# Key pieces turned in pairs in separate PSUM rooms, one fixed room for the output's two banks, and GpSimd's sums issued right behind its shares

## The chip, the cores and the metric

The kernel runs on one core of a Trainium2 chip. The metric is the time of one execution on the device in microseconds (us); the median of three runs is 544.29 us (543.98 to 544.59). The engines of the core work beside each other, each through its own instructions in order: TensorE (PE; its weight loads are counted apart as PEld), VectorE (DVE), ScalarE (ACT), GpSimd (POOL) and SyncE (SP), which issues nearly all DMAs.

## The reference

The inputs q, k, v have shape (B, H, S, D) = (2, 8, 576, 64), all in fp32. Attention with a computed bias is followed by two blocks of a mixture-of-experts shape, each without a router:

```python
scores = q @ k.T / sqrt(D)
x = (log1p(|i - j|) / log1p(max(i, 1)))[..., None]
bias = relu(x @ w1 + b1) @ w2            # hidden 32, one bias per head
attn = exp(scores + bias - max); attn /= attn.sum(-1) + 1e-9
y = attn @ v                             # to (1152, 512)
y = ((y @ w_a) * (y @ w_b)) @ w_out      # 512 -> 1536 -> 512
h = y @ w_in                             # 512 -> 1024
s = h * softmax(h)
out = (layernorm(s) * g_ln) @ w_out2     # 1024 -> 512
```

## The kernel before

Nearly every matrix product is made of three: each operand is split into a high part and the rest (`hi`, `lo`), both in the format fp32r, and hi·hi, hi·lo and lo·hi are summed in PSUM (`three`, L123 to L128). The high part is written by ACT, the rest by DVE as a difference.

PSUM has 8 banks. The pool `ps_s` (two buffers of two banks, tag `s`) holds scores, the bias sums `bps` and what lies beside them. `ps_t` (one buffer of two banks, tag `t`) holds turned (transposed) shares `pt` and turned pieces of q and k, `tp_...`. `ps_x` (two buffers of one bank) holds the attention's output `px_u` of one unit.

**The order of the work** is the order of the code: no scheduler moves anything, and each engine runs its instructions in program order. An instruction waits by semaphores for the tiles it reads and writes.

**Prologue** (loop from L511). The bias of a block of 128 rows is made in eight row groups T. `bias_hidden(T)` makes four relus of 128x576 each, on ACT (L360) or DVE (L362) as a letter string of the table HIDDEN says (`a` or `v`). `bias_sums` (L370) multiplies them by w2 on PE; `bias_out` copies the sums out (ACT, L380) and sends them by DMA from SP into the bias tile (L382). Beside it, pieces of q and k are turned by PE (`turn`, L275; a piece is one `piece`, L319) and split by `high` (ACT, L308) and `lower` (DVE, L313 for keys, L317 for queries). Three pieces are left over for the end of the prologue; the queries of the next unit and the keys of the second batch are fetched there by SP (L256, L261).

**Attention** (loop from L615). There are nine units u: eight of 128 rows of one batch, and a last one with the remaining 64 rows of both batches. A unit has four head pairs p, and step m of the loop starts pair m of 36. In a step stand: scores of two heads (L398); the next unit's queries turned; bias-add on DVE (L412) and exp on ACT (L419) of both heads; for the pair of the step before, `summed_powers`, a GpSimd instruction (sum + 1e-9, L424) and a DVE reciprocal of it (L425); then its `shares` on GpSimd (two multiplications of 128x576, L430); for the pair two steps before, the turning of its shares (L447) and the copies of them (L452, L461); the sums of a later row group T; `values` (L479) for the pair three steps before; the relus of T+1. After a unit's last pair ACT writes the high part of its output (xhi, L485), and one step later DVE the rest (xlo, L490). The first steps also turn the five key pieces of batch 1, at the end of steps 1, 1, 2, 2 and 3, one after another through `ps_t`. In steps 27 and 29 GpSimd clears rooms for the last unit's queries (`clear_q`, L285); from step 28 on the first weights of the next block are brought in and split (`first_one`: ACT L94 and L586, GpSimd L98 and L588, DVE L107, L109, L110).

**After attention** come the two other blocks (gated products `pm`, `po`, then `ph`, `pl`, `py`). The change does not touch them.

Of the kernel before, what the change touches and what calls it, by code (L numbers as in the profile page):

```python
# [17 lines left out]
P = 128  # L18
# [7 lines left out]

LAG = 2

HIDDEN = (("vvva", "vava", "vvva", "vavv", "vvva", "vavv", "vvva", "vavv"), ("vvav", "vvvv", "vavv", "vvva"))

LOADS = ((0, 1), (1, 1), (2, 2), (3, 2))
FIRST = ((-7, -5, -4, -1, 0, 1), (-6, -4, -2, 1, 2, 3), (-5, -2, 0, 3, 4, 5), (0, 2, 4, 6, 7, 8))
# [18 lines left out]
def tile_kernel(ctx, tc, q, k, v, w1, b1, w2, w_a, w_b, w_out, w_in2, w_out2, g_ln, psi, rpsi, out):  # L51
# [108 lines left out]
    with ExitStack() as actx:  # L160
# [6 lines left out]
        etp = actx.enter_context(tc.tile_pool(name="etp", bufs=2))  # L167
        sp = actx.enter_context(tc.tile_pool(name="sp", bufs=4))
        ps_t = actx.enter_context(tc.tile_pool(name="ps_t", bufs=1, space=PSUM))
        ps_x = actx.enter_context(tc.tile_pool(name="ps_x", bufs=2, space=PSUM))  # L170


        tabs = ac.tile([P, UW + NG], F32, name="tabs")
# [34 lines left out]
            return halves  # L208

        halves_r = table(half, UW - half, psi_r, half - 12, ps_s, "s")  # L210
        ps_nb = ps_x.tile([P, 4, NG // 4], F32, tag="x", name="ps_nb")
        for g in range(4):
            nc.tensor.matmul(ps_nb[g * HID:(g + 1) * HID], b1r, psi_i[:, :, g::4], start=True, stop=True)
        nc.scalar.copy(*halves_r[0])
# [5 lines left out]

        def scales():

            ps = ps_x.tile([P, 4, NG // 16], F32, tag="x", name="ps_rp")
            for c in range(4):
                for qd in range(4):
                    nc.tensor.matmul(ps[32 * qd:32 * qd + 32, c], order4[:, c].rearrange("p g h -> p (g h)"), rp_in[:, qd::4], start=True, stop=True)
            nc.scalar.copy(rp.rearrange("p (c k) -> p c k", c=4), ps)
# [78 lines left out]
        def high(views, by=1.0):  # L306
            for hi, _, ps in views:
                nc.scalar.activation(hi, ps, AF.Copy, scale=by)  # L308
# [7 lines left out]
                for l_, p_, h_ in parts_:  # L316
                    nc.vector.scalar_tensor_tensor(out=l_, in0=p_, scalar=by, in1=h_.bitcast(F32), op0=ALU.mult, op1=ALU.subtract)  # L317

        def piece(w, pool=ps_t, tag="t"):  # L319

            src, at, g, c = w
            ps = pool.tile([P, 2, 512], F32, tag=tag, name=f"tp_{'_'.join(map(str, w))}")
            nat = fetched[w]
            if src == "q":
                turn(ps, 0, nat, range(HG))
                return q_views(at, g, 0, ps, 0) + q_views(at, g, 1, ps, 2 * HF), -scale
            turn(ps, 0, nat, range(HG), (0, 1) if c < NK else (at,))
            return k_views(at, g, c, ps, 0), 1.0
# [36 lines left out]
        def bias_sums(T):  # L365

            bps = ps_s.tile([P, 2, 512], F32, tag="s", name=f"bps_{T}")
            for qd, h in enumerate(bias_w[T]):
                for a in range(2):
                    nc.tensor.matmul(bps[32 * qd:32 * qd + 32, a, 0:SH], w2bd, h[:, a * SH:(a + 1) * SH], start=True, stop=True)  # L370
            bias_w[T] = bps
# [49 lines left out]
        def summed_powers(u, p):  # L421
            sums, rec = st_[u]
            heads = slice(2 * p, 2 * p + 2)
            nc.gpsimd.tensor_scalar(rec[:, heads], sums[:, heads], 1e-9, 1.0, op0=ALU.add, op1=ALU.mult)  # L424
            nc.vector.reciprocal(rec[:, heads], rec[:, heads])  # L425

        def shares(u, h):
# [35 lines left out]
        def values(u, p):  # L463

            it, bs = units[u]
            if p == 0:
                st_["x", u] = ps_x.tile([P, HP, P], F32, tag="x", name=f"px_{u}")
            px = st_["x", u]
            et, ett = st_.pop(("et", u, p)), st_.pop(("ett", u, p))
            n = P // len(bs)  # L470
            for c in range(NC + 1):
                for j, part in ((j, part) for j in range(2) for part in range(2)):

                    rows = slice(j * D + part * HID, j * D + (part + 1) * HID)
                    for m, b in enumerate(bs):
                        cols = slice(m * n, (m + 1) * n)
                        lhsT = (vsb[:, b, c] if c < NC else vtl[:, b])[:, p, j, part * HID:(part + 1) * HID]
                        rhs = et[:, j * NC + c, cols] if c < NC else ett[:, cols]
                        nc.tensor.matmul(px[rows, p, cols], lhsT, rhs, start=(c == 0 and m == 0), stop=(c == NC), skip_group_check=True)  # L479
# [31 lines left out]
        for T in range(N0):  # L511
            bias_hidden(T)
            if T > 0:
                bias_sums(T - 1)
                bias_out(T - 1)
            if T == N0 - 2:
                halves_l = table(low, half - low, psi_l, low - 12, ps_t, "t")
            if T == N0 - 1:
                nc.scalar.copy(*halves_l[0])
                nc.vector.tensor_copy(*halves_l[1])  # L520
            if done:
                lower(*done)
                done = None
            if T > 0 and len(order) > 3:
                done = piece(order.pop(0))
                high(*done)
            if T == 1:
                for j in range(2):
                    nc.gpsimd.memset(vtl[(1 - j) * TL:(2 - j) * TL, :, :, j, :], 0.0)
        assert done is None and len(order) == 3  # L530
        bias_sums(N0 - 1)
        bias_out(N0 - 1)
        for w in ks[1][:2]:
            fetch(w)
        for g in range(2):
            fetch(("q", 1, g, 0))
        for p in range(-1, 2):
            load_v(0, p)
        for w in ks[1][2:]:
            fetch(w)  # L540
        for p in range(2, HP):
            load_v(0, p)
        bias_hidden(N0)
        made = piece(order[0])
        high(*made)
        lower(*made)
        made = piece(order[1])
        high(*made)
        lower(*made)
        bias_sums(N0)  # L550
        made = piece(order[2])
        high(*made)
        lower(*made)
        bias_out(N0)

        sums_at, keys_at, extra = {}, {}, {}
# [4 lines left out]
        for T in range(N0 + 1, S // 16):  # L561
            sums_at[T - N0 - 1] = T
        last_sums = max(sums_at)
        for m, w in zip((1, 1, 2, 2, 3), ks[1]):
            keys_at.setdefault(m, []).append(w)
        for p in range(-1, HP):
            later(2 * (2 + max(p, 0)), load_v, 1, p)
# [42 lines left out]
                f(*args)  # L610

        gone = []
        bias_hidden(sums_at[0])
        NP = len(pairs)
        for m in range(NP + LAG + 1):  # L615
            now = pairs[m] if m < NP else None
# [5 lines left out]
            if now:  # L622
                u, p = now
                scores(u, 2 * p)
                spare = scores(u, 2 * p + 1)
                if (u, p) in ((NU - 3, HP - 1), (NU - 2, 1)):
                    clear_q(NU - 1, NU - 2 - u == 0)
            elif up:
                spare = ps_s.tile([P, 2, 512], F32, tag="s", name=f"tails_{m}")
            if up:  # L630
# [7 lines left out]
                biased(u, 2 * p)  # L638
                powers(u, 2 * p)
            if last:  # L640
                summed_powers(*last)
            if now:
                biased(u, 2 * p + 1)
            if up:
                kept_tails(*up, spare)
            high(views, -scale)
# [20 lines left out]
            others(2 * m)  # L667
            if after is not None:
                bias_hidden(after)
            for w in keys_at.get(m, []):  # L670
                made = piece(w)
                high(*made)
                lower(*made)
            if out_ and out_[1] == HP - 1:
                inputs_high(out_[0])
                gone.append(out_[0])
# [345 lines left out]
```

## Time and profile before

| what | value |
|---|---|
| median of three runs | 544.29 us |
| the profiled execution | 545.0 us, of which the span of the trace is 543.2 us |
| PE busy | 510.3 us (94%) |
| DVE, ACT, POOL busy | 404.3, 280.9 and 143.0 us |
| mean granted TensorE clock | 0.971 of full speed |

A row of a timeline gives start, duration, engine, source line, operation, the tile it writes and those it reads, their shapes, the count, and in brackets how long the engine was idle just before it and what ended that. L412 is line 412 of the kernel before.

### The profile page before, as it was taken

The page shows a single profiled execution, that of the slowest core. Times are in us where ns is not written, and L with a number is a line of the kernel's source. Part 1 is how long each engine was busy: PE and PEld are TensorE (multiplying, and loading weights), DVE is VectorE, ACT ScalarE, POOL GpSimd, SP SyncE. Part 2 cuts the span into 40 slices and gives each one's busy share as a digit, 9 for nine tenths or more (in the row PEclk, how much of TensorE's full clock was granted, in tenths as well). Part 3 has the DMA queues.
Part 4 walks back from the last instruction along what each step waited for, and adds up shares of the span by engine and source line. Part 5 has one row for each costly group of instructions (what it writes and reads, how often), then busy time and mean ns, then how long its engine had stood idle before and what let it go on. Part 6 is the DMA issues. An engine that isn't in the chain of part 4 may idle for free.

```text
span 543.2 us, 13461 instructions
## 1 busy us (share of the span) xinstructions
PE 510.3 (94%) x5416; PEld 450.5 (83%) x5416; DVE 404.3 (74%) x880; ACT 280.9 (52%) x610; POOL 143.0 (26%) x216
## 2 busy tenths in 40 slices
PE   6768999999988889899999999999999999999997
PEld 3346777787767779899999999999999988888886
DVE  4777899999965853597899798897884466666561
ACT  5765888898875642455564334522534332232321
POOL 2012333343345560222222122242224330000000
PEclk9966999999988989999999999999999999999999
DMA  5886644434653100744444353445300000000011
GB/s 128 197 183 148 142 109 107 98 102 103 150 141 105 42 3 5 219 136 148 154 139 135 117 156 116 126 147 150 121 1 1 1 1 21 19 21 19 21 39 39
DMA packets 63520, 51.74 MB, mean 95 GB/s; under 512 B 41182, under 2 KB 53731, under 8 KB 63460
## 3 DMA queue, kind: packets, MB, share of 16 engines
q1 hardware_dynamic: 63184, 50.88, 34.8%
q8 instruction: 42, 0.69, 0.6%
q14 instruction: 18, 0.15, 0.1%
q10 hardware_dynamic: 276, 0.02, 0.0%
HBM read 36.73 MB, written 2.36 MB: 72 GB/s over the span
## 4 chain that ended last, share of the span: by engine, by line
PE 69%; DVE 9%; ACT 9%; DMA 4%; issue 4%; SPq 2%; POOL 1%; DVEq 0%; ACTq 0%
PE pm L128 26%; PE po L128 11%; PE py L919 9%; PE ph L859 9%; PE bps L370 4%; ACT e L419 3%; DVE h L362 3%; PE px L479 3%; PE s L398 2%; DMA nat_q<-in_q_dram 2%; PE pl L900 1%; PE pt L447 1%; DMA words<-in_moe_w_out_dram 1%; ACT qhi L308 1%; DVE e L412 1%
## 5 line engine op out<-in xcount | busy, mean ns | idle before, releaser
L128 PE MATMUL pm<-xhi,abh 128*128 128x384 f32 x240 | 80.2, 334 | 0.0
L128 PE MATMUL pm<-xhi,abl 128*128 128x384 f32 x240 | 80.2, 334 | 0.0
L128 PE MATMUL pm<-xlo,abh 128*128 128x384 f32 x240 | 80.2, 334 | 0.0
L98 POOL TENSOR_SCALAR f<-f 128x512 f32<-128x512 f32 x48 | 41.5, 865 | 142.7 <-ACT f L94 136.0
L430 POOL TENSOR_SCALAR e<-e,rec 128x576 f32<-128x576 f32 x72 | 52.9, 746 | 64.5 <-DVE rec L425 58.5
L419 ACT ACTIVATE e<-e,nm 128x576 f32<-128x576 f32 x72 | 56.2, 781 | 23.4 <-DVE rec L425 14.6
L412 DVE CUSTOM_DVE_ANT_0 e<-s,bias 128x576 f32<-128x576 f32 x72 | 53.9, 749 | 5.6 <-PE s L398 3.1
L362 DVE TENSOR_SCALAR h<-tabs 128x576 f32<-128x576 f32 x114 | 51.8, 515 | 0.7 <-PE bps L370 0.6
L370 PE MATMUL bps<-h,w2bd 128*32 128x288 f32 x576 | 47.0, 438 | 3.5 <-DVE nm L412 2.6
L128 PE MATMUL po<-gh,oh 128*128 128x384 f32 x144 | 48.5, 337 | 0.6 <-DVE x2s L790 0.6
L128 PE MATMUL po<-gh,ol 128*128 128x384 f32 x144 | 48.4, 336 | 0.0
L128 PE MATMUL po<-gl,oh 128*128 128x384 f32 x144 | 48.4, 336 | 0.0
L128 PEld LDWEIGHTS pm<-xhi,abh 128*128 128x128 f32 x240 | 45.1, 188 | 0.0
L128 PEld LDWEIGHTS pm<-xlo,abh 128*128 128x128 f32 x240 | 45.1, 188 | 0.0
L128 PEld LDWEIGHTS pm<-xhi,abl 128*128 128x128 f32 x240 | 45.1, 188 | 0.0
L110 DVE SCALAR_TENSOR_TENSOR f<-words,f 128x512 int32<-128x512 int32 x48 | 42.8, 891 | 1.6
L147 ACT COPY one<-pm 128x384 f32<-128x384 f32 x36 | 17.2, 478 | 50.2 <-PE pm L128 50.1
L94 ACT ACTIVATE f<-words 128x512 f32<-128x512 f32 x48 | 32.4, 675 | 18.6 <-DMA words<-in_moe_w_a_dram 7.4
L479 PE MATMUL px<-et,vsb 128*32 128x128 f32 (+1 forms) x1280 | 41.9, 276 | 0.0
L479 PEld LDWEIGHTS px<-et,vsb 128*32 128x32 f32 x1280 | 35.7, 116 | 5.9 <-issue 0.8
L874 ACT ACTIVATE ev<-ph,small 128x512 f32<-128x512 f32 x18 | 12.2, 684 | 49.7 <-DVE small L871 49.6
L109 DVE SCALAR_TENSOR_TENSOR f<-words,f 128x512 int32<-128x512 int32 x48 | 34.1, 710 | 1.3
(148 smaller groups left out, 1212.9 us busy)
## 6 DMA issues: line engine op xcount, KB each, us to landing
bias<-st SPq DMA_DIRECT2D x40, 288.0 KB, 3.7
words<-in_moe_w_out_dram SPq DMA_DIRECT2D x20, 512.0 KB, 3.5
words<-in_moe_w_a_dram SPq DMA_DIRECT2D x12, 512.0 KB, 3.6
words<-in_moe_w_b_dram SPq DMA_DIRECT2D x12, 512.0 KB, 3.8
nat_q<-in_q_dram SPq DMA_DIRECT2D x32, 128.0 KB, 3.5
words<-in_moe_w_in_dram SPq DMA_DIRECT2D x8, 512.0 KB, 3.6
arena<-in_k_dram SPq DMA_DIRECT2D x16, 128.0 KB, 2.6
vsb<-in_v_dram SPq DMA_DIRECT2D x16, 128.0 KB, 3.4
```

Source lines behind the costliest of these rows:

```text
L98: engine.tensor_scalar(f, f, WORD_MAX, WORD_MIN, op0=ALU.min, op1=ALU.max)
L109: nc.vector.scalar_tensor_tensor(out=b, in0=words[:, :, 1], scalar=-0x40000000, in1=b, op0=ALU.bitwise_and, op1=ALU.bitwise_or)
L110: nc.vector.scalar_tensor_tensor(out=b, in0=words[:, :, 0], scalar=29, in1=b, op0=ALU.logical_shift_right, op1=ALU.bitwise_or)
L128: nc.tensor.matmul(ps, w, x, start=(i == 0), stop=(i == n - 1))
L362: nc.vector.tensor_scalar(h, win, sc, 0.0, op0=ALU.add, op1=ALU.max)
L370: nc.tensor.matmul(bps[32 * qd:32 * qd + 32, a, 0:SH], w2bd, h[:, a * SH:(a + 1) * SH], start=True, stop=True)
L412: nc.vector.tensor_tensor_reduce(out=halves(e), in0=ps[:, :, 0:SH], in1=halves(bias_t[it][:, h, :]), op0=ALU.add, op1=ALU.min, scale=1.0, ...
L419: nc.scalar.activation(e, e, AF.Exp, bias=nm, scale=-1.0, accum_out=sums[:, h:h + 1])
L430: nc.gpsimd.tensor_scalar(e, e, rec[:, h:h + 1], 1.0, op0=ALU.mult, op1=ALU.mult)
L479: nc.tensor.matmul(px[rows, p, cols], lhsT, rhs, start=(c == 0 and m == 0), stop=(c == NC), skip_group_check=True)
L859: nc.tensor.matmul(ph[u][:, a], x[:, kc, cols], w[:, kc, a * 512:(a + 1) * 512], start=(i == 0), stop=(i == 3 * KD - 1))
L919: nc.tensor.matmul(ps, x[:, c, :], w[:, c, cols], start=(i == 0), stop=(i == 3 * KF - 1))
```

## The change

1. HIDDEN, the table of who makes which relu, gets other strings. From the second block of rows on, ACT makes four of 16 relus where it made three, two of them in one row group.
2. The pool `ps_x` becomes one fixed tile `xx` of two banks. Unit u's output lies in bank u%2 of it, and it also serves as a room for turned pieces: `piece` takes the name of a room, `t`, `x` or `s`.
3. In the prologue the next unit's queries are fetched earlier (T = 5), the three pieces left over are turned one after another into three rooms before the last bias sums and split behind them, and the relus of row group 9 move from ahead of the attention loop into its first step, behind both bias-adds. Both copies of the left half of the table go to DVE.
4. The key pieces of batch 1 come at steps 0, 0, 1, 1, 2. Their turning stands ahead of `values`, in the rooms `x` and `t`; their split stays at the end of the step.
5. `summed_powers` is split in two. GpSimd's sum is issued in the pair's own step, right behind the shares of the pair before and ahead of `clear_q` and the weights; the reciprocal (`inverted`) stays where it was, on DVE in the next step.

```diff
-HIDDEN = ((..., "vvva", ...), ("vvav", "vvvv", "vavv", "vvva"))
+HIDDEN = ((..., "vava", ...), ("vvvv", "vava", "vvav", "vavv"))
...
-        ps_x = actx.enter_context(tc.tile_pool(name="ps_x", bufs=2, space=PSUM))
+        ps_x = actx.enter_context(tc.tile_pool(name="ps_x", bufs=1, space=PSUM))
+        xx = ps_x.tile([P, 2, 512], F32, tag="x", name="xx")
...
-        def piece(w, pool=ps_t, tag="t"):
+        def piece(w, room="t"):
-            ps = pool.tile([P, 2, 512], F32, tag=tag, name=f"tp_{'_'.join(map(str, w))}")
+            ps = xx if room == "x" else (ps_t if room == "t" else ps_s).tile([P, 2, 512], F32, tag=room, ...)
...
+        def inverted(u, p):
+            _, rec = st_[u]
+            heads = slice(2 * p, 2 * p + 2)
             nc.vector.reciprocal(rec[:, heads], rec[:, heads])
...
-                st_["x", u] = ps_x.tile([P, HP, P], F32, tag="x", name=f"px_{u}")
+                st_["x", u] = xx[:, u % 2].rearrange("p (a t) -> p a t", a=HP)
...
+            if T == N0 - 3:
+                for g in range(2):
+                    fetch(("q", 1, g, 0))
...
-        bias_hidden(N0)
-        made = piece(order[0])
-        high(*made)
-        lower(*made)
-        made = piece(order[1])
-        high(*made)
-        lower(*made)
+        made = [piece(w, room) for w, room in zip(order, "txs")]
         bias_sums(N0)
-        made = piece(order[2])
-        high(*made)
-        lower(*made)
+        for w in made:
+            high(*w)
+            lower(*w)
...
-        for m, w in zip((1, 1, 2, 2, 3), ks[1]):
+        for m, w in zip((0, 0, 1, 1, 2), ks[1]):
...
             if last:
-                summed_powers(*last)
+                inverted(*last)
             if now:
                 biased(u, 2 * p + 1)
+            if m == 0:
+                bias_hidden(T)
...
                     shares(last[0], 2 * last[1] + h)
+            if now:
+                summed_powers(u, p)
+                if (u, p) in ((NU - 3, HP - 1), (NU - 2, 1)):
+                    clear_q(NU - 1, NU - 2 - u == 0)
...
+            made = [piece(w, room) for w, room in zip(keys_at.get(m, []), "xt")]
             if out_:
                 values(*out_)
...
-            for w in keys_at.get(m, []):
-                made = piece(w)
-                high(*made)
-                lower(*made)
+            for w in made:
+                high(*w)
+                lower(*w)
```

On DVE, from the end of the prologue to step 0's first bias-add (`ISA e_0...`), the order was this; `h_0` to `h_3` are relus, `klo` the rest of a key piece:

```order
L362 TENSOR_SCALAR h_3_438<-tabs 128x576
L317 SCALAR_TENSOR_TENSOR qlo_1_0_450<-tp_q_1_0_440,qhi_1_0_449 128x128 x4
L313 TENSOR_TENSOR klo<-tp_k_1_0_457,khi 128x2x4x64
L313 TENSOR_TENSOR klo<-tp_k_1_1_477,khi 128x2x4x64
L362 TENSOR_SCALAR h_0_492<-tabs 128x576
L362 TENSOR_SCALAR h_1_494<-tabs 128x576
L362 TENSOR_SCALAR h_2_496<-tabs 128x576
L362 TENSOR_SCALAR h_3_498<-tabs 128x576
L412 ISA e_0_522,nm_0_523<-s_0_502,bias_209 128x576
```

The same place now:

```order
L363 TENSOR_SCALAR h_3_403<-tabs 128x576
L318 SCALAR_TENSOR_TENSOR qlo_1_0_449<-tp_q_1_0_439,qhi_1_0_448 128x128 x4
L314 TENSOR_TENSOR klo<-xx,khi 128x2x4x64
L314 TENSOR_TENSOR klo<-tp_k_1_1_458,khi 128x2x4x64
L413 ISA e_0_512,nm_0_513<-s_0_492,bias_208 128x576
```

The four relus of row group 9 no longer stand ahead of the first bias-add.

On GpSimd, in steps 27 to 30, the order was this; `rec<-sums` is the sum with 1e-9, `e<-e,rec` two shares, MEMSET the clearing:

```order
L424 TENSOR_SCALAR rec_2848<-sums_2847 128x2
L430 TENSOR_SCALAR e_6_3170<-e_6_3170,rec_2848 128x576 x2
L285 MEMSET qhi_True_3333 128x512
L285 MEMSET qlo_True_3334 128x512
L285 MEMSET qhi_True_3337 128x512
L285 MEMSET qlo_True_3338 128x512
L424 TENSOR_SCALAR rec_3239<-sums_3238 128x2
L430 TENSOR_SCALAR e_0_3260<-e_0_3260,rec_3239 128x576 x2
L98 TENSOR_SCALAR single_3406<-single_3406 128x512
L424 TENSOR_SCALAR rec_3239<-sums_3238 128x2
L430 TENSOR_SCALAR e_2_3347<-e_2_3347,rec_3239 128x576 x2
```

The same place now:

```order
L425 TENSOR_SCALAR rec_3228<-sums_3227 128x2
L435 TENSOR_SCALAR e_0_3249<-e_0_3249,rec_3228 128x576 x2
L425 TENSOR_SCALAR rec_3228<-sums_3227 128x2
L286 MEMSET qhi_True_3343 128x512
L286 MEMSET qlo_True_3344 128x512
L286 MEMSET qhi_True_3347 128x512
L286 MEMSET qlo_True_3348 128x512
L98 TENSOR_SCALAR single_3395<-single_3395 128x512
L435 TENSOR_SCALAR e_2_3328<-e_2_3328,rec_3228 128x576 x2
L425 TENSOR_SCALAR rec_3228<-sums_3227 128x2
L98 TENSOR_SCALAR single_3478<-single_3478 128x512
```

Each sum now stands ahead of the memsets and of the weight work (L98), and the shares of the next pair (`e_2`) stand behind both.

On DVE, at the end of a unit in the fourth step of its period, with the semaphores waited for, the order was this:

```order
L317 SCALAR_TENSOR_TENSOR qlo_1_0_1063<-s_7_1153,qhi_1_0_1062 128x128
L490 TENSOR_TENSOR xlo<-px_789,xhi 128x4x128
L362 TENSOR_SCALAR h_0_1237<-tabs 128x576 [waits DVE_49]
L362 TENSOR_SCALAR h_1_1239<-tabs 128x576 [waits DVE_49]
L362 TENSOR_SCALAR h_2_1241<-tabs 128x576 [waits DVE_49]
```

The same place now:

```order
L318 SCALAR_TENSOR_TENSOR qlo_1_0_1058<-s_7_1148,qhi_1_0_1057 128x128
L495 TENSOR_TENSOR xlo<-xx,xhi 128x4x128 [waits PE_49]
L363 TENSOR_SCALAR h_0_1231<-tabs 128x576 [waits DVE_49]
L363 TENSOR_SCALAR h_2_1235<-tabs 128x576 [waits DVE_49]
L413 ISA e_0_1266,nm_0_1267<-s_0_1244,bias_486 128x576 [waits DMAHW2_49,DMAHW3_49,DMAHW1_49,DMAHW4_49,DMAHW0_49,DMAHW6_49,DVE_49,PE_49]
```

One relu has left DVE there, and xlo now waits for PE: `xx` is followed as one tile, so the reading of one bank waits for the values of the next unit written ahead of it into the other.

## Rows read from the trace of the kernel before

**Rows 1.** The page, part 1: busy time, share and instructions of each engine.

```profile
PE 510.3 (94%) x5416; PEld 450.5 (83%) x5416; DVE 404.3 (74%) x880; ACT 280.9 (52%) x610; POOL 143.0 (26%) x216
```

**Rows 2.** Windows: length, PE, PEld, DVE, ACT, POOL busy, clock, DMA share, GB/s.

```profile
27.60:60.65 33.05, 26.04 (x346) 18.95 (x344) 24.02 (x63) 20.64 (x46) 7.16 (x13) 0.70 0.73 158
60.65:153.42 92.77, 88.76 (x1984) 72.23 (x1984) 87.88 (x250) 83.11 (x199) 37.25 (x67) 1.00 0.50 116
163.13:196.67 33.54, 28.03 (x595) 23.96 (x591) 23.00 (x59) 20.58 (x54) 19.52 (x31) 0.91 0.18 58
196.67:216.00 19.33, 19.33 (x354) 18.17 (x351) 6.70 (x12) 6.60 (x16) 4.27 (x6) 0.98 0.01 3
```

**Rows 3.** Timeline of DVE, end of the prologue to step 4.

```profile
28.51 0.69 DVE L313 TENSOR_TENSOR klo<-tp_k,khi 128x512 fp32r<-128x512 f32 x1 [1.42 <-ACT khi L308]
...
30.84 0.75 DVE L412 CUSTOM_DVE_ANT_0 e<-s,bias 128x576 f32<-128x576 f32 x1
...
35.00 0.76 DVE L412 CUSTOM_DVE_ANT_0 e<-s,bias 128x576 f32<-128x576 f32 x1
...
42.70 0.75 DVE L412 CUSTOM_DVE_ANT_0 e<-s,bias 128x576 f32<-128x576 f32 x1
...
56.77 0.75 DVE L412 CUSTOM_DVE_ANT_0 e<-s,bias 128x576 f32<-128x576 f32 x1
...
60.65 0.75 DVE L412 CUSTOM_DVE_ANT_0 e<-s,bias 128x576 f32<-128x576 f32 x1
```

**Rows 4.** Timeline of all engines, the second key piece of step 1.

```profile
40.72 0.69 PE L275 MATMUL tp_k<-ident,arena 64*128 64x64 f32 x8 [2.57 <-DVE klo L313]
...
41.46 0.60 ACT L308 ACTIVATE khi<-tp_k 128x512 fp32r<-128x512 f32 x1 [1.51 <-PE tp_k L275]
```

**Rows 5.** Timeline of SP, the DMA issues at the end of the prologue.

```profile
20.14 3.35 SPq L382 DMA_DIRECT2D bias<-st  x3
...
26.04 3.06 SPq L256 DMA_DIRECT2D nat_q<-in_q_dram  x4
```

**Rows 6.** The page, part 6: issues of bias rows, KB each, us to landing.

```profile
bias<-st SPq DMA_DIRECT2D x40, 288.0 KB, 3.7
```

**Rows 7.** The page, part 5: relus on DVE and shares on GpSimd.

```profile
L430 POOL TENSOR_SCALAR e<-e,rec 128x576 f32<-128x576 f32 x72 | 52.9, 746 | 64.5 <-DVE rec L425 58.5
...
L362 DVE TENSOR_SCALAR h<-tabs 128x576 f32<-128x576 f32 x114 | 51.8, 515 | 0.7 <-PE bps L370 0.6
```

**Rows 8.** Windows over one period of four steps, columns as in rows 2.

```profile
107.81:111.69 3.88, 3.10 (x68) 2.38 (x68) 3.79 (x12) 3.02 (x8) 1.66 (x3) 1.00 0.63 139
111.69:115.61 3.92, 3.92 (x94) 3.28 (x94) 3.83 (x12) 3.88 (x11) 1.66 (x3) 1.00 0.31 79
115.61:119.50 3.89, 3.89 (x94) 3.25 (x92) 3.80 (x12) 3.81 (x10) 1.66 (x3) 1.00 0.31 80
119.50:124.75 5.25, 5.19 (x118) 4.22 (x116) 4.83 (x14) 4.36 (x11) 1.66 (x3) 1.00 0.46 112
```

**Rows 9.** Line 360, relus on ACT: ns minimum/median/maximum, first and last start.

```profile
L360 ACT ACTIVATE h<-tabs x30: 759/796/805, 6.5 to 149.5; 128x576 f32<-128x576 f32 x30
```

**Rows 10.** Waits from 152 to 200 us: in total, times, longest.

```profile
DVE rec L425 <- POOL rec L424: 10.1, 7, 2.0
```

**Rows 11.** Timeline of all engines, steps 27 to 30.

```profile
155.02 0.17 DVE L425 RECIPROCAL rec<-rec 128x2 f32<-128x2 f32 x1 [0.83 <-POOL rec L424]
...
159.12 0.24 PE L275 MATMUL s<-ident,nat_q 64*128 64x64 f32 x1 [1.19 <-DMA nat_q<-in_q_dram]
...
164.23 0.53 POOL L285 MEMSET qhi_True<- 128x512 f32 x1 [4.25 <-PE s L398]
...
169.94 0.61 POOL L98 TENSOR_SCALAR single<-single 128x512 f32<-128x512 f32 x1 [1.76 <-ACT single L94]
```

**Rows 12.** Line 588, GpSimd's difference of the first weights, columns as in rows 9.

```profile
L588 POOL TENSOR_TENSOR first<-single,first x4: 1272/1278/1510, 183.5 to 200.8; 128x512 fp32r<-128x512 f32 x4
```

**Rows 13.** Line 110, DVE's last word operation, columns as in rows 9.

```profile
L110 DVE SCALAR_TENSOR_TENSOR single<-words,single x4: 693/693/982, 178.9 to 198.5; 128x512 int32<-128x512 int32 x4
```

More of the change, by code (lines that the diff above doesn't have):

```diff
@@ L27 @@
 LAG = 2
-HIDDEN = (("vvva", "vava", "vvva", "vavv", "vvva", "vavv", "vvva", "vavv"), ("vvav", "vvvv", "vavv", "vvva"))
+HIDDEN = (("vvva", "vava", "vava", "vavv", "vvva", "vavv", "vvva", "vavv"), ("vvvv", "vava", "vvav", "vavv"))
 LOADS = ((0, 1), (1, 1), (2, 2), (3, 2))
@@ L210, in tile_kernel @@
         halves_r = table(half, UW - half, psi_r, half - 12, ps_s, "s")
-        ps_nb = ps_x.tile([P, 4, NG // 4], F32, tag="x", name="ps_nb")
+        ps_nb = xx[:, 0, 0:NG].rearrange("p (c k) -> p c k", c=4)
         for g in range(4):
@@ L221, in scales @@
         def scales():
-            ps = ps_x.tile([P, 4, NG // 16], F32, tag="x", name="ps_rp")
+            ps = xx[:, 1, 0:NG // 4].rearrange("p (c k) -> p c k", c=4)
             for c in range(4):
@@ L317, in lower @@
                     nc.vector.scalar_tensor_tensor(out=l_, in0=p_, scalar=by, in1=h_.bitcast(F32), op0=ALU.mult, op1=ALU.subtract)
-        def piece(w, pool=ps_t, tag="t"):
+        def piece(w, room="t"):
             src, at, g, c = w
-            ps = pool.tile([P, 2, 512], F32, tag=tag, name=f"tp_{'_'.join(map(str, w))}")
+            ps = xx if room == "x" else (ps_t if room == "t" else ps_s).tile([P, 2, 512], F32, tag=room, name=f"tp_{'_'.join(map(str, w))}")
             nat = fetched[w]
@@ L517, in tile_kernel @@
                 halves_l = table(low, half - low, psi_l, low - 12, ps_t, "t")
-            if T == N0 - 1:
-                nc.scalar.copy(*halves_l[0])
-                nc.vector.tensor_copy(*halves_l[1])
             if done:
@@ L529, in tile_kernel @@
                     nc.gpsimd.memset(vtl[(1 - j) * TL:(2 - j) * TL, :, :, j, :], 0.0)
+            if T == N0 - 3:
+                for g in range(2):
+                    fetch(("q", 1, g, 0))
         assert done is None and len(order) == 3
+        for half_l in halves_l:
+            nc.vector.tensor_copy(*half_l)
+        bias_hidden(N0)
         bias_sums(N0 - 1)
         bias_out(N0 - 1)
-        for w in ks[1][:2]:
+        for w in ks[1][:3]:
             fetch(w)
-        for g in range(2):
-            fetch(("q", 1, g, 0))
         for p in range(-1, 2):
             load_v(0, p)
-        for w in ks[1][2:]:
+        for w in ks[1][3:]:
             fetch(w)
@@ L612, in tile_kernel @@
         gone = []
-        bias_hidden(sums_at[0])
         NP = len(pairs)
@@ L625, in tile_kernel @@
                 spare = scores(u, 2 * p + 1)
-                if (u, p) in ((NU - 3, HP - 1), (NU - 2, 1)):
-                    clear_q(NU - 1, NU - 2 - u == 0)
             elif up:
```

## The prediction

> **What bounds the kernel now.** I read the page's busy times first. PE is busy for 510.3 us of 543.2 [rows 1], so all that the change can win lies in the 33 us in which PE stands, plus what PE does at the half clock. Then I cut the span into windows and looked in each for the engine that is full [rows 2]. The reader is to see four stages. From 27.6 to 60.65 (steps 0 to 3) no engine is full: PE 26.0 of 33.1 us and at a granted clock of 0.70, DVE 24.0, ACT 20.6; something makes them wait in turn. From 60.65 to 153.42 PE (88.8), DVE (87.9) and ACT (83.1) are all nearly full in 92.8 us. From 163 to 196.67 again no engine is full, with PE at 28.0 of 33.5 and GpSimd, elsewhere idle, at 19.5. From 196.67 on PE works 19.33 of 19.33 us: whatever is won before that point is carried whole to the end, and the change touches nothing behind it.
>
> In the first stage the timeline names the chain: a key piece is turned by PE, PE then waits 2.57 us until DVE has done the rest of the piece before, since both use one room, and ACT waits 1.51 us for PE [rows 4]; the next bias-add comes behind that [rows 3]. In the third stage the list of waits has a wait of DVE's reciprocal for GpSimd's sum, 10.1 us in seven [rows 10]; one of them is the 0.83 in step 27, so six with 9.3 us lie behind 163 [rows 11].
>
> The profiled execution took 545.0 us, 0.7 above the median of 544.3. I sum up against the profile and take 0.7 off at the end.
>
> **The head (items 3 and 4).** Before, the first bias-add starts at 30.84 and the one of step 4 at 60.65 [rows 3], 29.81 later.
> - *Start.* The four relus of row group 9, from 29.20 (28.51 + 0.69) to 30.84, 1.64 us, go from ahead of that bias-add, and so does the turn through one room that makes DVE wait 1.42 us for the last key piece [rows 3]. Alone that gives 30.84 - 1.64 - 1.42 = 27.8. But the bias-add waits for the last bias rows. SP issues them at the end of its three issues, at 23.5 at the latest, and they land 3.7 us later at the median [rows 5, 6]; the query fetch of four issues and 3.06 us that I find behind them at 26.04 [rows 5] now stands ahead of them on SP. There SP mostly waits: three issues in 3.35 us are 1.12 each, where one of the query fetch is 3.06 / 4 = 0.77 [rows 5], so I count nearly all of the fetch as lying in waits of SP: last issue about 23.6, landing 27.3 to 28.3 in a stretch with the DMA engines 0.73 busy [rows 2]. I take 28.3, 2.5 earlier; the ends are 27.8 and 30.8 (the fetch costs its full 3.06).
> - *Step 0* was 4.16 (30.84 to 35.00 [rows 3]). Two key pieces come in: 2 x 0.60 on ACT [rows 4] and two relus of 0.80 on ACT (the other two on DVE) [rows 9] make 2.8 on ACT; of the two turnings, 2 x 0.69 on PE [rows 4], I count 1.0, as the rest lies beside DVE. So 8.0.
> - *Step 1* has two more pieces. A step without pieces is 3.9 [rows 8]; 2 x 0.60 on ACT and the last 0.69 on DVE [rows 3, 4] make it 5.8; the waits of 2.57 and 1.51 do not return, since the two pieces have two rooms and PE turns them ahead of the values. *Step 2* has one piece: 3.9 + 0.60 + 0.69 = 5.2. *Step 3* has none, 3.9. *Step 4* is 4.9 in place of 3.88, as the fetched queries and ACT, which lags from step 0, come due there.
> - Sum: 28.3 + 8.0 + 5.8 + 5.2 + 3.9 + 4.9 = 56.1, and 0.5 for PE at the half clock in step 3, 56.6 in place of 60.65: **-4.05**. Ends: -6 (start at 27.8, steps 0 and 1 each 0.7 less) and -1.5 (start at 30.8).
>
> **The steady period (items 1 and 2).** One period of four steps takes 3.88 + 3.92 + 3.89 + 5.25 = 16.94, and DVE is the fullest engine in the short ones [rows 8]. A relu that leaves or enters DVE moves it by 0.43 or so (1.64 for four, above; 0.515 with its fill [rows 7]). One of the short steps gets a relu more on DVE, 4.31. The long one, which holds xlo, gets two fewer: 5.25 - 0.86 = 4.39. There xlo gets a wait for the values of the next unit; behind it on DVE are two relus and the next bias-add. PE is nearly full in that step (5.19), so the values end late; I take 0.2 for it. Sum: 4.31 + 4.59 + 3.88 + 3.88 = 16.66, 0.28 less, in five periods (steps 6 to 25): **-1.5** with rounding. Ends: 0 (the two relus of ACT, 1.6, hold up its copies) and -4 (PE's own 16.10 per period is the floor, 0.84 x 5).
>
> **Step 27 (item 5).** Its reciprocal no longer waits 0.83 us, but step 28 waits 1.19 us for the queries' DMA [rows 11], which is on no path that the sum shortens: **0**. The memsets, which wait 4.25 us for PE to let go of their room [rows 11], now wait behind the sum.
>
> **The tail (item 5).** The six waits, 9.3 us [rows 10, 11], go, as each sum is issued a step earlier, as soon as the exps are done. What is late next is GpSimd's queue, since what stood behind the sum now stands ahead of the next shares. In step 31 these come behind four memsets of 0.53 and a weight operation of 0.61 [rows 11]: I count 0.7 on PE, whose turning waits for the shares. The sum for step 30's pair then stands behind those shares, two of 0.746 [rows 7]: 0.85 on DVE. Toward the end the difference of 1.28 [rows 12] stands ahead of shares and sum: 0.75 on DVE and 1.1 on PE in step 35. So 9.3 - 3.4 = 5.9. Following the new order forward with each row's duration, I get the last values of step 35 at 190.0 in place of 196.67, 6.7. I take **-6.2**. No more than 8.5 can go: PE has 28.03 of work there, 3.0 of it owed to the clock of 0.91 (0.09 x 33.54 [rows 2]), so 25.0 of 33.5 stay. The other end is -3, half of the sum, if each freed wait meets another.
>
> The granted clock is 0.70 in the head and 0.91 in the tail [rows 2]; it is low where PE had been standing, and with shorter waits it should rise, which is not counted but in the ends.
>
> A rule that speaks against the change bears on the tail: with shares pulled beside DVE's word operations, the two engines may stand in each other's way. The row: DVE's last word operation takes 0.693 us at the least and at the median of four, and 0.982 at most [rows 13]. The Trainium skill, "SBUF — State Buffer", section "Who interferes with whom", says that a DVE instruction with two SBUF inputs contends with a GpSimd instruction that reads SBUF, and that whoever issues first has the shared ports for its whole length. By that rule more of these would go to 0.982; without it they stay.
>
> Sum: -4.05 - 1.5 - 6.2 = -11.75, so 533.25 in a profiled execution, **532.5** as a median.
>
> **Rivals.**
> - *The tail is given back in GpSimd's queue.* For it: GpSimd is at 19.5 of 33.5 us there [rows 2], and 0.29 (0.982 - 0.693 [rows 13]) more on each of seven word operations with two inputs is 2.0 on DVE. Against: DVE has 23.0 of 33.5 busy [rows 2]. With -3 in place of -6.2: 544.3 - 4.05 - 1.5 - 3 = 535.7.
> - *The head wins nothing.* The bias rows or the keys land late, as the query fetch stands ahead of them, and PE stays at the half clock through step 3. For it: DMA share 0.73 and clock 0.70 [rows 2]. Against: the waits of 2.57 and 1.51 [rows 4] are not of DMA. 544.3 - 1.5 - 6.2 = 536.6.
> - *The new shares of relus do nothing*, since ACT is as full as DVE: 3.81 to 3.88 in two short steps [rows 8]. But ACT's sum over the period is 15.07, and 15.07 + 0.80 is still under 16.66. 544.3 - 4.05 - 6.2 = 534.0.
> - *Slower: the one room `xx`.* It is followed whole, so at each unit's end PE's values wait for xhi on ACT, xhi waits behind ACT's relus, and xlo on DVE waits for those values. If ACT lags by the 1.6 us of its two relus [rows 9], all three engines stand in turn at eight unit ends. From 11.75 / 8 = 1.5 us at each it eats the whole gain; at 2.0 it costs 16: 544.3 - 11.75 + 16 = 548.5. Against: xhi has the scores and the sums of the next step, over 2 us, before the values come due.
>
> **How the numbers follow.** A measurement of this kernel can tell about 0.2%, 1.1 us, from no change. Chances: the forecast 0.58, the tail given back 0.13, the head without gain 0.14, relus without gain 0.07, slower by `xx` 0.08. The likeliest is 532.5. The range: upward it takes in the first three rivals and half of the head's and the tail's upper ends, 539.0; downward half of the way to the lower ends (-6, -4, -8.5: 525.8), 527.5. All cases but the last are faster by far more than 1.1: 0.90 with the part of the last in which the price stays under 1.4; within 0.2% 0.04; slower 0.06.
>
> **What would show it.** Right: the bias-add of step 4 at 56 to 57 and no wait of a turned key piece for klo; a period of 16.6 to 16.7; no wait of the reciprocal for the sum behind step 27, or one under 1 us in all but steps 31 and 35; the last scores of step 35 some 11 to 12 earlier and PE full behind them. Wrong: waits of px for xhi or of xlo for px of over 1 us in every unit (the room); a first bias-add at 30 or later that waits for a DMA; GpSimd's shares late behind L98 and L588, with PE waiting for them at L447.

## The result, and the profile after

The changed kernel takes 536.5 us (median of four runs, 535.69 to 537.36) where the kernel before takes 544.14: a ratio of 0.9858, 95% interval 0.9841 to 0.9875. The profiled execution took 536.58 us, its span 534.5 in place of 543.2, 8.7 less. I cut both spans at the same points, at the first scores matmul of steps 5, 27 and 29, at the first gated product behind attention, and at the end.

| stretch | before | after | difference | forecast |
|---|---|---|---|---|
| to step 5 | 59.81 | 59.03 | -0.78 | -4.05 |
| steps 5 to 26 | 92.90 | 92.14 | -0.76 | -1.5 |
| steps 27 and 28 | 10.42 | 10.70 | +0.28 | 0 |
| step 29 to the first gated product | 33.54 | 27.30 | -6.24 | -6.2 |
| behind it | 346.5 | 345.3 | -1.2 | 0 |

The page of the changed kernel, part 1, to be held against [rows 1]:

```profile
PE 504.0 (94%) x5416; PEld 446.1 (83%) x5416; DVE 401.3 (75%) x873; ACT 285.2 (53%) x617; POOL 143.7 (27%) x216
```

PE has lost 6.3 us of busy time with the same 5416 matmuls: it ran less at the half clock (mean granted clock 0.983, before 0.971). The windows of the changed kernel, columns as in [rows 2]:

```profile
25.72:59.03 33.31, 22.32 (x331) 16.11 (x332) 21.34 (x58) 20.36 (x46) 7.19 (x13) 0.80 0.77 166
59.03:151.17 92.14, 88.41 (x1984) 72.28 (x1980) 86.66 (x246) 86.95 (x204) 36.66 (x66) 1.00 0.51 117
154.09:161.87 7.78, 5.07 (x79) 4.03 (x76) 3.74 (x11) 3.90 (x11) 4.03 (x9) 0.78 0.64 145
161.87:189.17 27.30, 24.83 (x594) 21.53 (x590) 23.50 (x59) 20.96 (x55) 19.98 (x30) 1.00 0.21 67
```

The head (steps 0 to 4) begins 1.9 us earlier than before and ends 0.8 earlier, so it is longer, 33.31 us in place of 32.21, and PE still stands for a third of it. In the tail PE is busy for 24.8 of 27.3 us at the full clock. Step 28 (third row) stayed as bad as it was in the kernel before:

```profile
155.62:163.13 7.51, 4.99 (x79) 3.88 (x75) 4.63 (x14) 4.49 (x13) 2.78 (x5) 0.79 0.59 135
```

**The head.** DVE's timeline in the changed kernel, the first bias-adds of steps 0, 1, 2, 4 and 5, as in [rows 3]:

```profile
31.02 0.76 DVE L413 CUSTOM_DVE_ANT_0 e<-s,bias 128x576 f32<-128x576 f32 x1 [5.35 <-DMA arena<-in_k_dram]
...
39.37 0.75 DVE L413 CUSTOM_DVE_ANT_0 e<-s,bias 128x576 f32<-128x576 f32 x1
...
44.75 0.75 DVE L413 CUSTOM_DVE_ANT_0 e<-s,bias 128x576 f32<-128x576 f32 x1
...
53.80 0.76 DVE L413 CUSTOM_DVE_ANT_0 e<-s,bias 128x576 f32<-128x576 f32 x1 [0.20 <-PE s L399]
...
59.74 0.76 DVE L413 CUSTOM_DVE_ANT_0 e<-s,bias 128x576 f32<-128x576 f32 x1
```

DVE is done 5.35 us before it may start; the four relus that stood ahead of the first bias-add have gone, and it starts as late as before (30.84). The releaser named, the keys' transfer, is inferred from the event that came last; of the transfers the instruction needs only the bias rows, which were issued right ahead of the keys. SP's timeline shows the order of the issues:

```profile
19.51 2.47 SPq L257 DMA_DIRECT2D nat_q<-in_q_dram  x4
22.07 2.42 SPq L383 DMA_DIRECT2D bias<-st  x3
24.55 2.91 SPq L262 DMA_DIRECT2D arena<-in_k_dram  x4
```

The last bias issue ends at 24.49, 1.0 later than before [rows 5], and 6.5 us ahead of the bias-add. The DMA view of 20 to 36 us (KB each, median us from issue to landing) tells of the landings; for the bias rows of the changed kernel it gives none. The changed kernel:

```profile
arena<-in_k_dram SPq DMA_DIRECT2D x5, 128.0 KB, 5.5
nat_q<-in_q_dram SPq DMA_DIRECT2D x4, 128.0 KB, 6.2
```

and the kernel before in the same window:

```profile
arena<-in_k_dram SPq DMA_DIRECT2D x7, 128.0 KB, 4.7
bias<-st SPq DMA_DIRECT2D x3, 288.0 KB, 4.2
nat_q<-in_q_dram SPq DMA_DIRECT2D x4, 128.0 KB, 3.8
```

The queries land 6.2 us after their issue in place of 3.8. That what was issued behind them waited in the DMA engines is argued here; the first experiments test it.

**The period** of four steps in the changed kernel, columns as in [rows 8], cut at the first scores matmul of steps 16 to 20 (rows 8 are cut some 2 us later in a step, so only the sums compare):

```profile
104.90:109.52 4.62, 4.13 (x96) 3.31 (x92) 4.42 (x13) 4.51 (x11) 1.67 (x4) 1.00 0.48 103
109.52:113.57 4.05, 4.05 (x94) 3.29 (x90) 3.96 (x13) 4.01 (x10) 1.82 (x4) 1.00 0.43 107
113.57:117.46 3.89, 3.89 (x94) 3.25 (x90) 3.80 (x12) 3.81 (x10) 1.64 (x3) 1.00 0.29 76
117.46:121.64 4.18, 4.01 (x95) 3.32 (x92) 3.73 (x11) 3.52 (x10) 1.54 (x4) 1.00 0.52 125
```

16.74 in place of 16.94. Steps 12 to 15 win as much (16.73), but steps 8 to 11 and 20 to 23 win nothing (17.18 and 16.96, before 17.14 and 16.96), and the whole stretch from step 5 to 26 is only 0.76 shorter. The wait that the fixed room makes is there, 2.8 us in six units (line 495, xlo):

```profile
its engine sat idle before it (us, times) until:
  PE xx L484: 2.8, 6
```

**The tail.** Of the reciprocal's waits for the sum [rows 10], two are left in the changed kernel from 150 to 196 us, both at the places named (steps 31 and 35):

```profile
DVE rec L430 <- POOL rec L425: 2.0, 2, 1.0
```

### The profile page after: what moved, and what is told of

It reads as the page before. It is cut to its first block, busy times and chain, and to the rows that moved or that the text cites. A ratio compares the mean times of both kernels' runs of the same rounds, so it can differ in the third digit from the quotient of the medians.

```text
span 534.5 us, 13462 instructions
## 1 busy us (share of the span) xinstructions
PE 504.0 (94%) x5416; PEld 446.1 (83%) x5416; DVE 401.3 (75%) x873; ACT 285.2 (53%) x617; POOL 143.7 (27%) x216
## 4 chain that ended last, share of the span: by engine, by line
PE 74%; DVE 8%; ACT 7%; DMA 5%; issue 4%; SPq 1%; POOL 1%; DVEq 0%; ACTq 0%
PE pm L128 27%; PE po L128 14%; PE py L922 9%; PE ph L862 9%; PE bps L371 5%; PE xx L484 3%; DVE h L363 3%; ACT e L420 3%; DMA nat_q<-in_q_dram 2%; DVE e L413 2%; PE pl L903 1%; PE s L399 1%; PE pt L452 1%; DMA words<-in_moe_w_out_dram 1%; ACT qhi L309 1%
## 5 line engine op out<-in xcount | busy, mean ns | idle before, releaser
L98 POOL TENSOR_SCALAR f<-f 128x512 f32<-128x512 f32 x48 | 41.4, 862 | 141.8 <-ACT f L94 117.3
L371 PE MATMUL bps<-h,w2bd 128*32 128x288 f32 x576 | 48.2, 438 | 11.1 <-DVE h L363 6.5
L363 DVE TENSOR_SCALAR h<-tabs 128x576 f32<-128x576 f32 x106 | 48.5, 514 | 1.0 <-PE bps L371 0.8
L110 DVE SCALAR_TENSOR_TENSOR f<-words,f 128x512 int32<-128x512 int32 x48 | 42.9, 895 | 1.6
L484 PE MATMUL xx<-et,vsb 128*32 128x128 f32 (+1 forms) x1280 | 40.1, 267 | 0.0
L371 PEld LDWEIGHTS bps<-h,w2bd 128*32 128x32 f32 x576 | 20.0, 114 | 23.4 <-issue 8.8
L484 PEld LDWEIGHTS xx<-et,vsb 128*32 128x32 f32 x1280 | 34.1, 111 | 5.5 <-issue 0.2
```

The source lines that it names most:

```text
L98: engine.tensor_scalar(f, f, WORD_MAX, WORD_MIN, op0=ALU.min, op1=ALU.max)
L110: nc.vector.scalar_tensor_tensor(out=b, in0=words[:, :, 0], scalar=29, in1=b, op0=ALU.logical_shift_right, op1=ALU.bitwise_or)
L363: nc.vector.tensor_scalar(h, win, sc, 0.0, op0=ALU.add, op1=ALU.max)
```

## The experiments

Each was run on a chip together with runs of the kernel before, and a ratio is to those. Two kernels whose ratios differ by under 0.4% are not told apart by their times; there the traces speak.

**What holds up the first bias-add.** The first experiment moves the query fetch behind the bias rows, the second only its second half; the third leaves it and empties the queue behind the bias rows.

```diff
-            if T == N0 - 3:
-                for g in range(2):
-                    fetch(("q", 1, g, 0))
...
         bias_out(N0 - 1)
+        fetch(("q", 1, 0, 0))
         for w in ks[1][:3]:
             fetch(w)
         for p in range(-1, 2):
             load_v(0, p)
+        fetch(("q", 1, 1, 0))
```

> The changed kernel, with the fetch of the next unit's queries moved: its first half behind the last bias row issue and ahead of the keys, its second half behind the first values. Theory A (the first bias-add starts at 31.0 because the bias rows lie behind the four query transfers in the DMA queue): the last bias rows land by 27.5, the first bias-add starts at 27 to 28, step 1's scores start at 33 to 34 in place of 37.0, and the whole is 2 to 4 us shorter than the changed kernel (532.5 to 534.5). Rival B (the transfers issued behind the bias rows, keys and values, take the bandwidth): the bias-add starts at 30 or later and the whole stays at 536 to 537. Rival C (the wait moves to the queries or keys, since the bytes needed before step 1 are the same): the first bias-add starts at 28, but step 1 at 36 or later, whole 536.

For the second, `fetch(("q", 1, 0, 0))` stays at T = 5 and the other half follows the first keys.

> The changed kernel, with only the first half of the queries' fetch (two of four transfers) ahead of the last three bias rows and the second half behind the first keys. Theory A: half of the delay, the first bias-add at 29 to 29.7 in place of 31.0, the whole 1 to 2 us shorter than the changed kernel. Rival B: no change of the first bias-add, 31.0.

```diff
-        for w in ks[1][:3]:
-            fetch(w)
...
+            if m == 0:
+                for w in ks[1]:
+                    fetch(w)
+                for p_ in range(-1, HP):
+                    load_v(0, p_)
```

> The changed kernel, with the query fetch where the change put it (ahead of the last three bias rows), but with every transfer that was issued right behind those rows (keys of batch 1, values of batch 0) moved to the end of step 0, and the key pieces to steps 2, 2, 3, 3, 4. Only the start of the first bias-add is of interest. Theory A: it stays at 30 to 31, since the queries are still ahead. Rival B: it starts at 27 to 28.5, as nothing takes the bandwidth from the bias rows. The total time should be longer, as values and keys come late.

In the third kernel key pieces and the first unit's output overwrite each other in one room from step 3 on, so only what lies ahead is read, and its time (544.7 in one run) is not compared. The first bias-add on DVE's timeline, in this order: q_behind, q_half, loads_late.

```profile
28.39 0.76 DVE L413 CUSTOM_DVE_ANT_0 e<-s,bias 128x576 f32<-128x576 f32 x1 [2.72 <-DMA nat_q<-in_q_dram]
```

```profile
29.35 0.76 DVE L413 CUSTOM_DVE_ANT_0 e<-s,bias 128x576 f32<-128x576 f32 x1 [3.44 <-DMA bias<-st]
```

```profile
31.13 0.76 DVE L413 CUSTOM_DVE_ANT_0 e<-s,bias 128x576 f32<-128x576 f32 x1 [5.48 <-issue]
```

With four, two and no query transfers ahead of the bias rows it starts at 31.02, 29.35 and 28.39; with the queue behind them empty it starts no earlier (31.13). So theory A stands and B falls. Of the 2.6 us between the ends 0.9 is the issue itself (the last of the bias rows' issues ends at 24.49, 24.18 and 23.57) and the rest is the landing: the DMA view of 20 to 36 us gives the bias rows 6.2 us in q_half, 4.6 in q_behind and 4.2 in the kernel before. The times do not follow: q_behind 535.3 (0.9838, 0.9787 to 0.9889), less gain than A expected, q_half 533.9 (0.9817, 0.9775 to 0.9859), more; the intervals of both overlap that of the changed kernel. C is half right: in q_behind step 1 starts at 34.2, but step 4 takes 7.6 us in place of 5.9. Its wait for the third unit's queries is as long as in the changed kernel (1.72 and 1.65), but PE's granted clock is 0.78 there in place of 1.00.

**What each part is worth, undone or alone.** Item 5 undone, then item 5 alone on the kernel before:

```diff
             if last:
+                summed_powers(*last)
                 inverted(*last)
...
-            if now:
-                summed_powers(u, p)
-                if (u, p) in ((NU - 3, HP - 1), (NU - 2, 1)):
-                    clear_q(NU - 1, NU - 2 - u == 0)
```

> The changed kernel with item 5 undone (GpSimd's sum issued one step later, behind clear_q and the weight work, as before). If the tail's gain is item 5's: the waits of the reciprocal for the sum are back (six or seven, 9 to 10 us), the stretch from step 29 to the first gated product behind attention is 33 to 34 us long in place of 27.3, and the whole is 6 to 7 us longer than the changed kernel (542.5 to 543.5). Rival: the tail is shorter for another reason (the clock, or an earlier arrival at it), and the whole stays within 2 us of 536.5.

> The kernel before with item 5 alone (GpSimd's sums right behind its shares, ahead of clear_q and the weights). If the tail's gain is item 5's alone and does not need the others: the stretch from step 29 to the first gated product is 27.3 us in place of 33.5, the whole 538 to 539.5 (5 to 6 less than the kernel before). Rival: it needs an earlier arrival or the other shares of relus, and the whole is 541 to 544.

Undone: 541.6 (0.9967, 0.9944 to 0.999), 5.1 more than the changed kernel (5.9 by the ratios), with seven waits of 10.0 us in total again. That is under the 6 to 7 expected: in its profiled execution the tail is 5.8 longer, but step 28 is 1.7 shorter (6.05, at a granted clock of 1.00). Its window from step 29 to the first gated product:

```profile
159.74:192.85 33.11, 26.89 (x595) 22.78 (x591) 22.75 (x59) 21.64 (x56) 18.92 (x30) 0.95 0.21 67
```

Alone: 537.3 (0.9899, 0.9863 to 0.9934), better than expected. Its step 28 and the stretch behind:

```profile
155.26:161.23 5.97, 3.55 (x78) 2.84 (x75) 3.31 (x10) 2.81 (x9) 3.81 (x8) 1.00 0.58 125
161.23:188.47 27.24, 24.92 (x594) 21.59 (x590) 23.97 (x62) 22.11 (x58) 20.11 (x31) 1.00 0.26 81
```

The tail's gain is item 5's alone: 33.1 with it undone, 27.2 with it alone. And it is most of the change: the other four items together bring the ratio from 0.9899 to 0.9858, and the two intervals overlap, so the times alone do not show that those four win anything.

Item 1 undone (the old strings), and item 2's room taken apart behind the key pieces:

```diff
-HIDDEN = ((..., "vava", ...), ("vvvv", "vava", "vvav", "vavv"))
+HIDDEN = ((..., "vvva", ...), ("vvav", "vvvv", "vavv", "vvva"))
```

> The changed kernel with item 1 undone (the old strings of relus). Theory (the prediction's, 0.28 us a period, of which the traces showed 0.19): the period goes from 16.75 back to some 16.95 to 17.2 (the wait of xlo now comes on top of the old step of 5.08) and the whole is 1 to 2 us longer than the changed kernel, 537.5 to 538.5. Rival: ACT gives as much as DVE gets, no difference, 536 to 537.

```diff
-                st_["x", u] = xx[:, u % 2].rearrange("p (a t) -> p a t", a=HP)
+                if not px_pool:
+                    xctx.close()
+                    px_pool.append(actx.enter_context(tc.tile_pool(name="px", bufs=2, space=PSUM)))
+                st_["x", u] = px_pool[0].tile([P, HP, P], F32, tag="x", name=f"px_{u}")
```

> The changed kernel, but from the first unit's output on with two rooms of one bank each in place of the fixed room of two (the key pieces still use the two banks as one room before). Theory: the 0.23 us by which the fourth step of each period is longer than in the kernel before (4.15 to 4.18 in place of 3.92) is xlo's wait for the values of the next unit, which the fixed room makes; without it that step is back at 3.9 and the whole is 1 to 1.6 us shorter than the changed kernel (535.0 to 535.5). Rival: that step is longer since its relus were moved, and nothing changes (536.5).

relus_back: 538.6 (0.9895, 0.9866 to 0.9924). two_rooms: 536.35 (0.9854, 0.9825 to 0.9883), no faster, where 1 to 1.6 less was expected. Of the two periods (steps 16 to 19) the step that holds xlo, relus_back first and two_rooms second:

```profile
105.81:111.28 5.47, 4.25 (x94) 3.31 (x90) 5.27 (x15) 3.31 (x10) 1.69 (x4) 1.00 0.53 114
```

```profile
104.39:108.94 4.55, 4.55 (x95) 3.65 (x91) 4.13 (x13) 4.55 (x11) 1.81 (x4) 1.00 0.46 97
108.94:112.84 3.90, 3.90 (x92) 3.27 (x91) 3.81 (x12) 3.83 (x10) 1.66 (x3) 1.00 0.48 118
```

The periods: 16.94 before; 17.35 with the fixed room and the old strings; 16.74 with both new; 16.50 with the new strings and two rooms. So in this period the fixed room costs 0.24 to 0.41 and the strings win 0.44 to 0.61. The expectation named the wrong step: without the fixed room the gain is in the two steps shown (4.62 and 4.05 in the changed kernel), and the fourth stays at 4.15. By the traces two_rooms is 1.33 shorter from step 5 to 27; its steps 28 and 29 take 0.7 of that, and the stretch behind attention the rest.

Items 3 and 4 undone:

```diff
-        made = [piece(w, room) for w, room in zip(order, "txs")]
+        bias_hidden(N0)
+        made = piece(order[0])
+        high(*made)
+        lower(*made)
...
-        for m, w in zip((0, 0, 1, 1, 2), ks[1]):
+        for m, w in zip((1, 1, 2, 2, 3), ks[1]):
```

> The changed kernel with items 3 and 4 undone: the key pieces of batch 1 one after another through one room at steps 1, 1, 2, 2, 3, the prologue's last pieces, the relus of row group 9 and the query fetch as in the kernel before; the fixed room, the sums and the relu strings stay. Theory: the head's gain was almost eaten by the late bias rows, 0.8 to 1 us at step 5, so this is 0.5 to 1.5 us longer than the changed kernel (537 to 538). Rival: items 3 and 4 cost more than they bring, and this is faster (under 536).

538.0 (0.9885, 0.9854 to 0.9916), 1.5 more than the changed kernel, as expected; but the intervals overlap, and in its profiled execution step 5 starts only 0.5 later (59.53), so the size is not settled.

**The transfers.** PE's two waits for queries in the changed kernel, in steps 4 and 28, on its timeline:

```profile
56.03 0.34 PE L276 MATMUL s<-ident,nat_q 64*128 64x64 f32 x4 [1.65 <-DMA nat_q<-in_q_dram]
...
158.00 0.84 PE L276 MATMUL s<-ident,nat_q 64*128 64x64 f32 x4 [2.56 <-DMA nat_q<-in_q_dram]
```

The next kernel changes only transfers' places, beside the move of q_behind:

```diff
-            later(2 * (2 + max(p, 0)), load_v, 1, p)
+            later(2 * (3 + max(p, 0)), load_v, 1, p)
...
-            if now and p > 1 and u + 2 < NU:
-                fetch(("q", u + 2, p - 2, 0))
+            if now and u + 2 < NU and 0 <= (p if u else p - 2) < 2:
+                fetch(("q", u + 2, p if u else p - 2, 0))
```

> The changed kernel with three transfers' places changed: the queries of the second unit behind the bias rows (as in q_behind), the values of batch 1 one step later, so that they stand behind the queries of the third unit and not ahead, and from the second unit on the queries fetched two steps earlier. Theory: the waits of PE for queries go, 1.7 us in step 4 and 2.6 us in step 28, on top of the 2.6 us by which the first bias-add of q_behind is earlier: 530.5 to 532.5. Rival: the DMA engines are full in the head and the wait only moves to another transfer: 533.5 to 535.5, as q_behind and q_half.

528.1 (0.9705, 0.9675 to 0.9735), 8.4 less than the changed kernel and 2.4 less than the best expected. Its windows: the head, step 28, and from step 29 on:

```profile
25.71:55.04 29.33, 21.58 (x330) 15.66 (x330) 21.16 (x58) 20.06 (x46) 7.16 (x13) 0.83 0.79 168
149.74:152.87 3.13, 3.13 (x80) 2.71 (x76) 3.09 (x9) 2.47 (x9) 2.55 (x7) 1.00 0.67 180
152.87:180.39 27.52, 25.16 (x594) 21.58 (x590) 24.55 (x61) 22.41 (x59) 21.34 (x33) 1.00 0.25 80
```

The head is 4.0 shorter, step 28 4.6. For the head the move of q_behind alone is not enough: with it the head takes 32.67, as the wait in step 4 stays. What the last hunk does is told by that hunk alone, on the changed kernel and on the kernel before:

> The changed kernel with only one of best_one's three parts: from the second unit on the queries are fetched two steps earlier. Theory: step 28 goes from 7.8 to 3.1 to 3.5 us as in best_one, the head stays (first bias-add at 31.0, step 4 with its wait for queries): 531.5 to 533. Rival: step 28 was short in best_one since the head's loads were spread otherwise, 535 to 536.5.

> The kernel before, with nothing of the change, but from the second unit on with the queries fetched two steps earlier (as in queries_early). Theory: the wait for the last unit's queries and the half clock behind it were in the kernel before as well, where the change could not reach them; step 28 goes from 7.5 to 3.2 to 4 us there too, and the whole is 3.5 to 4.5 us shorter than before (539.5 to 540.5). Rival: there the reciprocal's wait for the sum in the same steps takes the wait's place, step 28 stays over 5.5, and the whole gains 2 at most.

532.0 (0.979, 0.9762 to 0.9817) and 540.2 (0.994, 0.9918 to 0.9962): 4.5 and 3.8 less by the medians, 3.7 and 3.3 by the ratios. Step 28, on the changed kernel and on the kernel before:

```profile
153.67:156.81 3.14, 3.14 (x79) 2.69 (x75) 3.10 (x9) 2.48 (x9) 2.57 (x7) 1.00 0.65 176
```

```profile
154.55:158.64 4.09, 3.16 (x80) 2.69 (x76) 3.99 (x12) 3.06 (x11) 2.52 (x5) 1.00 0.56 142
```

So the wait for the last unit's queries was in the kernel before, and no part of the change reached it. Last, best_one with two_rooms' edit:

> best_one with the two separate rooms for the output. Theory: the 0.22 us a period that two_rooms won in steps 5 to 27 was lost again in its wait for the last unit's queries (step 28) and is kept now that they are early: 526.5 to 527.5, against 528.1 for best_one. Rival: another wait at the end of attention takes it, 528.

527.8 (0.9708, 0.968 to 0.9736), just above the expected. In the traces it is 1.2 shorter up to the first gated product (179.19 and 180.39), and the times cannot tell it from best_one. Both beat the changed kernel and the kernel before.

## Why the prediction was right, and where it was not

- **The whole** is 4.0 above the forecast of 532.5, 3.3 of it from the head. That 536.5 stands beside the 536.6 of the rival "the head wins nothing" is in part luck: the head did win 0.8, the steady stretch half of its 1.5, and the 1.2 behind attention were in no sum. (Half of the way from 532.5 to 525.8 would put the range's lower end at 529.2, not at 527.5; nothing here hangs on it.)
- **The tail held** in its mechanism: the two waits left are where GpSimd's queue was said to be late. That the size fits, 6.24 where 6.2 was forecast, is in part luck, as the sum left out the clock: PE's busy time there fell from 28.03 to 24.83 us while its granted clock rose from 0.91 to 1.00, and with 28.03 us of work in PE no more than 5.5 could have gone. The word operation that the rule on shared ports spoke of did not change (0.691, 0.692 and 0.983 us; [rows 13] has 0.693, 0.693 and 0.982):

```profile
L110 DVE SCALAR_TENSOR_TENSOR single<-words,single x4: 691/692/983, 174.4 to 190.8; 128x512 int32<-128x512 int32 x4
```

But the operation ahead of it (L109), which reads two tiles as well, took 0.69, 0.67, 1.20 and 0.76 us where it took 0.69, 0.67, 0.94 and 0.68. In both kernels each of these operations that began while a GpSimd instruction had 0.2 us or more still to run is long (0.76 to 1.20), and no other is. So the rows agree with that rule, but the two operations take 0.3 us more than before in the whole tail and not the rival's 2.0.

- **The head failed in its step "Start"**: "so I count nearly all of the fetch as lying in waits of SP: last issue about 23.6, landing 27.3 to 28.3". The issues end at 24.49, so the fetch cost SP 0.9 more than the forecast counted. The larger error, 1.8, is the landing: I took the median from issue to landing [rows 6] as if it did not depend on what was issued ahead. The first bias-add is 2.7 later than forecast, and is the sign named for being wrong, one at 30 or later that waits for a DMA; q_half gives back 1.7 of it and q_behind 2.6. What happened is the rival in which the head wins nothing, for the first reason it gave; the other, PE at the half clock through step 3, did not come (granted clock 0.89 in step 3, before 0.59). (The bias-add at 60.65 that the prediction calls step 4's is step 5's; its working counts all five steps.)
- The next three terms of the head were right: steps 0, 1 and 2 took 8.35, 5.38 and 5.32 (8.0, 5.8 and 5.2 forecast). Step 3 took 3.73, without the 0.5 that I added for the half clock. Step 4 took 5.94 and not 4.9: the third unit's queries are fetched behind the values of batch 1, and PE waits 1.65 for them.
- **The period** won 0.20 at its best and not 0.28: 0.44 by the strings (0.48 forecast) and -0.24 by xlo's wait (-0.20), which falls mostly on the step behind it and not on its own. Behind xlo DVE makes two relus in place of four, as the prediction counts (two relus have left it there, and not the one that the text below the order lists names). Over the five periods the forecast 1.5 came to 0.76, and why steps 8 to 11 and 20 to 23 win nothing is open.
- **Step 27 was right**: the 0.83 went, and in step 28 PE's waits for queries grew from 1.58 to 2.56 us. I did not ask what that wait itself was worth; with the half clock that comes with it, it was some 4 us, the most that one edit took off the changed kernel.
- **Behind attention** I forecast nothing, and 1.2 went. 0.4 is the clock at its start, 0.8 a shorter wait of PE for a gated product on DVE (L148: 1.41 us before, 0.61 after). Rows of before, then of after:

```profile
196.67:201.17 4.50, 4.50 (x27) 4.50 (x24) 2.52 (x5) 2.12 (x5) 3.34 (x6) 0.91 0.00 0
219.83:239.57 19.74, 18.33 (x105) 18.01 (x105) 16.15 (x28) 11.18 (x21) 5.62 (x8) 1.00 0.58 180
```

```profile
189.17:193.27 4.10, 4.10 (x28) 4.10 (x24) 2.13 (x4) 1.33 (x4) 3.10 (x6) 1.00 0.00 0
211.93:230.86 18.93, 18.32 (x105) 18.00 (x105) 16.15 (x28) 10.72 (x21) 5.62 (x8) 1.00 0.59 187
```

  The second pair says little of the change: that wait is 0.54 us in q_half and 1.83 in q_behind, kernels that do not differ there, so that the stretch takes 18.9 to 20.1 us.

## What to carry to other kernels

A transfer that is moved ahead of others on one issuing queue costs the others its time in the DMA engines as well as its issue; here four transfers of 128 KB cost the bias rows 2.6 us, 1.7 of it behind the issue. Ask for each transfer what must land first, and issue in that order. A wait that comes just behind the one removed is worth pricing by itself; here the wait for one unit's queries, which the change did not touch, held some 4 us in two lines of code. One tile over two banks is followed as one: it ties a reader of one bank to the writer of the other (0.47 us for each of xlo's six waits here).

## What the runs showed of the hardware that was not expected

- **The DMA queue.** Four, two and no transfers of 128 KB ahead put the first bias-add at 31.02, 29.35 and 28.39: 1.0 us for the first two and 1.7 for the next two, the later issue included. The Trainium skill, "DMA: Bandwidth & Descriptors", section "Queues, rings and completion order", says that SP's DMAs share one ring on each of the DMA engines and that each engine consumes its descriptors in ring order; these three starts, and the 31.13 with nothing behind, agree.
- **One wait, two prices.** Step 28 waits for the queries' DMA in the kernel before, in the changed kernel and with item 5 alone. In the first two PE needs 4.99 and 5.07 us for its work at a granted clock of 0.79 and 0.78, in the third 3.55 us at 1.00, after a wait of 2.1 us. Step 4 shows the same pair: 4.28 us of work at 1.00 in the changed kernel, 5.87 at 0.78 in q_behind, after waits of 1.65 and 1.72. Which of them it will be, the rows do not tell; it is worth some 1.5 us, and it goes with the wait.
